# Query sketch of two batches through DRAM: one factor repeated by a read-back, the other on TensorE

## The chip, the core and the metric

The kernel runs on one core of a Trainium2 chip. A core has TensorE (PE in the profile; its weight loads are PEld), VectorE (DVE), ScalarE (ACT), GpSimd (POOL) and SyncE (SP), each with an instruction queue of its own that runs in order, and DMA queues that share 16 DMA engines. The metric is the time of one execution on the device in microseconds, as the median of several runs. Beside it stands one profiled execution with a trace of every instruction.

## The reference

```python
# q, k, v: (4 batches, 4 heads, 1088 tokens, 32), S1, S2: (8, 32)
def phi(x):                                # 32 numbers of a token become 64
    a = einsum('rd,bhsd->bhsr', S1, x)
    b = einsum('rd,bhsd->bhsr', S2, x)
    return einsum('bhsi,bhsj->bhsij', a, b).reshape(*x.shape[:-1], 64)
q_p, k_p = phi(q), phi(k)
kv = einsum('bhsf,bhsd->bhfd', k_p, v)
z = sum(k_p, axis=2)
num = einsum('bhsf,bhfd->bhsd', q_p, kv)
den = einsum('bhsf,bhf->bhs', q_p, z)[..., None] + 1e-6
x = (num / den).transpose(0, 2, 1, 3).reshape(4352, 128)
out = maximum(x @ w_in, 0)**2 @ w_out      # w_in 128x2048, w_out 2048x128
```

A linear attention with a sketch of degree two, and a feed-forward net (FFN) with the square of a ReLU on its result. All of it is one kernel.

## The kernel before

The four batches (b = 0 to 3 in the code, batches 1 to 4 in words) go one after the other through the attention, and the FFN works on tiles of 512 or 256 tokens as soon as these have passed it. Much of the attention of one batch therefore lies among FFN work of the batches ahead.

**Attention of a batch.** `kin`, `qin`, `vin` and `vtl` are loaded from DRAM. Those of batch 1 come in pieces on the queues of SP and ACT. All others, and the weights `w_in` and `w_out` in four pieces each, come through POOL (L360). DVE transposes `kin` to `kT` (L476) and `qin` to `qT` (L562). PE multiplies `kT` by `SK`, the sketch matrices (L496, a buffer `a` or `h`); ACT copies the first factor to `ka` (L509), and `kb` for POOL (L511); DVE or POOL forms all 64 products of a token, `kp` (L521). PE sums `kp` times `vp` over the tokens (L538). `vp` is `vin` with a column of ones, copied by ACT or POOL (L461, L464). Four copies put the sum into `kvz` (L553).

**The query side.** PE multiplies `qT` by `SR`, the sketch matrix with every row repeated eight times, once for each of the two factors (L583). Each factor thus arrives in PSUM already as 64 rows per head, one in the order 11112222 and one in the order 12341234. ACT copies the first factor to `A` (L598), since only one operand of the product is to come from PSUM, and DVE multiplies the other by it into `qp` (L609). PE forms `num`, with the sum for `den` in column 33 (L629). DVE adds eps (L647, L650), takes the reciprocal `rec` (L651) and multiplies it in, `xs` (L652, L656). PE transposes (L671), and DVE or ACT copies to `xT` (L677).

**FFN of a tile.** PE: `h` = `w_in` by `xT` (L698). ACT or DVE: `r` = relu(h) (L707, L709). DVE or ACT: `g` = r*r (L717, L715). PE: `o` sums `w_out` by `g` over all 2,048 inner rows (L724). DVE transposes to `osb` (L731), and SP stores (L741).

**Buffers.** PSUM holds three `h` of 1,024 columns, one `a` and one `o` of 512. SBUF holds four `r`, four `g`, three `osb`, three sets `den`/`rec`/`xs` and three `A`. Inputs of a batch have two sets, used in turn.

**Order.** The program is not written in order. Every piece is an operation with its engines, a duration that the author assumed, its inputs and its buffers. `Graph.run` plays these through once and emits the instructions in the order in which the operations start in that plan. Among operations that can start at about the same time a list `RANK` decides, and `SIDE` fixes the engine of those that could run on either. On the chip each engine then keeps that order and waits by semaphores.

**Loads.** A POOL load waits on a *gate*. The first (L346) is a one-column copy of the last piece of `vin` of batch 1. After that, the third load back must have landed: POOL copies one number of it to `gt` (L359). For batches 3 and 4 a further gate (L663) waits until the first `xs` of the batch ahead exists. 30 matmuls of zeros, `wz` (L325), fill PE before the data is there.

Of the kernel before, what the change touches and what calls it, by code (L numbers as in the profile page):

```python
# [9 lines left out]
F32 = mybir.dt.float32  # L10
# [9 lines left out]
DGE = 0.43  # L20


RANK = [
    165, 170, 191, 487, 140, 473, 83, 243, 387, 29, 569, 257, 275, 598, 621, 607, 623, 611, 618, 608, 596, 594,
    599, 602, 595, 610, 616, 617, 600, 605, 612, 614, 597, 609, 606, 603, 620, 619, 601, 613, 604, 622, 615,
    121, 85, 496, 286, 292, 31, 53, 582, 435, 476, 79, 120, 298, 526, 415, 475, 574, 355, 338, 160, 178, 10, 14,
    133, 365, 141, 57, 69, 104, 5, 2, 103, 126, 345, 26, 12, 306, 247, 314, 150, 9, 44, 152, 164, 71, 222, 4,
    74, 3, 55, 6, 100, 7, 93, 403, 182, 173, 507, 114, 539, 293, 76, 261, 80, 447, 384, 111, 215, 225, 366, 221,
    276, 299, 394, 17, 78, 92, 39, 145, 1, 135, 203, 193, 15, 98, 64, 52, 313, 382, 389, 357, 130, 369, 401,
    466, 212, 144, 579, 391, 370, 552, 456, 244, 518, 572, 327, 283, 498, 495, 530, 516, 262, 418, 591, 352,  # L30
    368, 564, 543, 485, 348, 477, 575, 316, 465, 302, 437, 542, 310, 188, 479, 201, 440, 49, 263, 147, 129, 199,
    67, 143, 11, 360, 367, 587, 511, 430, 450, 205, 541, 115, 59, 245, 464, 241, 482, 36, 171, 207, 444, 340,
    279, 537, 555, 218, 336, 86, 557, 109, 51, 554, 571, 66, 346, 406, 463, 264, 38, 489, 424, 124, 236, 25,
    250, 439, 371, 46, 350, 200, 392, 514, 154, 118, 8, 198, 18, 297, 206, 290, 524, 474, 462, 565, 592, 404,
    488, 139, 153, 142, 122, 374, 256, 134, 284, 27, 533, 81, 491, 535, 87, 556, 334, 443, 405, 106, 269, 326,
    268, 235, 540, 523, 503, 472, 460, 159, 578, 454, 397, 508, 558, 228, 41, 445, 509, 347, 23, 343, 300, 586,
    224, 291, 469, 471, 213, 28, 285, 20, 88, 50, 589, 77, 242, 33, 240, 132, 68, 398, 237, 204, 500, 90, 321,
    116, 515, 195, 289, 548, 303, 180, 184, 425, 412, 251, 234, 520, 429, 416, 156, 547, 329, 341, 317, 576,
    566, 560, 455, 502, 220, 380, 528, 480, 223, 181, 30, 32, 43, 75, 65, 166, 232, 22, 190, 499, 315, 97, 70,
    501, 72, 434, 127, 570, 417, 119, 158, 174, 373, 157, 253, 332, 484, 230, 214, 101, 532, 301, 238, 162, 216,  # L40
    231, 24, 378, 312, 172, 113, 358, 421, 82, 13, 359, 478, 529, 402, 255, 123, 442, 274, 61, 419, 559, 258,
    361, 45, 567, 536, 265, 525, 550, 545, 308, 395, 505, 583, 531, 325, 385, 590, 427, 335, 457, 110, 295, 519,
    561, 323, 544, 35, 73, 330, 62, 60, 233, 137, 91, 148, 63, 337, 48, 208, 95, 185, 146, 42, 458, 187, 112,
    167, 107, 163, 420, 58, 196, 287, 108, 149, 89, 362, 99, 331, 461, 383, 219, 410, 339, 483, 381, 273, 272,
    517, 259, 254, 436, 451, 534, 551, 319, 549, 584, 270, 356, 21, 453, 280, 490, 414, 553, 376, 521, 294, 396,
    581, 510, 513, 512, 282, 296, 426, 568, 131, 364, 438, 375, 94, 342, 136, 16, 278, 19, 209, 309, 486, 176,
    84, 56, 408, 177, 179, 493, 239, 105, 151, 311, 573, 40, 372, 432, 400, 47, 227, 192, 267, 102, 379, 328,
    585, 407, 377, 304, 506, 422, 563, 271, 189, 305, 527, 96, 428, 459, 186, 117, 217, 522, 37, 54, 388, 288,
    333, 210, 468, 399, 494, 229, 318, 183, 175, 249, 349, 413, 393, 277, 128, 562, 169, 252, 260, 497, 441,
    449, 588, 577, 593, 324, 246, 467, 452, 281, 322, 34, 492, 226, 307, 344, 125, 138, 353, 248, 538, 446, 433,  # L50
    155, 0, 431, 211, 390, 202, 351, 363, 386, 580, 546, 470, 409, 354, 481, 197, 423, 320, 411, 448, 266, 168,
    194, 504, 161,
# [3 lines left out]
    10: 1, 72: 1, 73: 0, 74: 1, 88: 1, 93: 1, 94: 0, 95: 1, 121: 1, 130: 0, 132: 0, 151: 0, 152: 1, 153: 0,  # L56
    174: 1, 178: 0, 187: 1, 188: 1, 202: 1, 207: 0, 208: 0, 209: 1, 210: 1, 234: 0, 242: 1, 244: 0, 258: 1,
    263: 1, 264: 1, 266: 0, 285: 0, 289: 1, 292: 1, 295: 0, 299: 1, 300: 1, 303: 0, 304: 0, 312: 1, 313: 0,
    316: 0, 317: 0, 320: 1, 324: 0, 328: 0, 329: 0, 332: 0, 333: 0, 336: 0, 337: 1, 341: 1, 349: 0, 350: 0,
    353: 0, 357: 0, 358: 0, 361: 0, 362: 1, 365: 0, 369: 0, 370: 0, 373: 1, 374: 0, 378: 1, 390: 0, 391: 1,  # L60
    395: 1, 398: 1, 399: 0, 403: 1, 406: 0, 407: 1, 410: 1, 411: 1, 414: 0, 415: 0, 418: 1, 419: 0, 427: 0,
    436: 1, 439: 0, 440: 0, 443: 0, 444: 0, 447: 0, 448: 0, 452: 0, 456: 1, 468: 0, 469: 0, 473: 1, 476: 0,
    480: 0, 481: 0, 484: 1, 485: 0, 488: 1, 492: 0, 496: 0, 505: 0, 506: 0, 509: 0, 510: 0, 513: 0, 518: 1,
    522: 1, 525: 0, 529: 0, 530: 0, 533: 1, 534: 0, 555: 1, 558: 0, 559: 0, 562: 0, 563: 0, 566: 0, 567: 1,
    571: 0, 574: 1, 584: 0, 587: 0, 592: 0, 595: 1, 604: 0, 608: 0, 609: 0, 613: 0, 616: 0, 617: 1,
# [10 lines left out]
class Op:  # L76
    def __init__(self, name, alts, fn, deps, pri, alloc, uses, port, dma, after, extra):
        self.extra = extra
        self.name, self.alts, self.fn, self.pri = name, alts, fn, pri
        self.deps = [d for d in deps if d is not None]  # L80
        self.alloc, self.uses, self.port, self.dma = alloc, uses, port, dma
        self.after = [d for d in after if d is not None]
        self.look = LOOK
        self.start = self.end = self.eng = None


class Graph:
# [22 lines left out]
    def run(self):  # L110
        eng_free, port_free, pipe, dge = {}, 0.0, 0.0, 0.0
        lanes = []
        todo = {id(o): len(o.deps) + len(o.after) for o in self.ops}
# [6 lines left out]
        while ready:  # L120
            cands = []
            for o in ready:
# [13 lines left out]
                for e, (busy, lat, *pen) in o.alts.items():  # L136
                    pen = pen[0] if pen else 0.0
                    t = max(eng_free.get(e, 0.0), t_slot)
# [30 lines left out]
            eng_free[e] = t + busy  # L169
            if e in o.port:  # L170
                port_free = t + busy
# [32 lines left out]
def kernel(  # L204
# [25 lines left out]

    def T(name, shape, dt=F32):
        return sb.tile(shape, dt, name=name, tag=name)
# [42 lines left out]
    kb = T("kb", [128, 2, H, R])  # L275
    kp = [T(f"kp{i}", [128, NJ, H, F]) for i in range(NB)]
    kvz = [[T(f"kvz{i}{x}", [128, 2, 2, D + 1]) for x in range(2)] for i in range(NB)]
    qp = [T(f"qp{i}", [128, 2, S]) for i in range(NB)]

# [39 lines left out]

    o_wz = add("wz", {"DVE": dve(256)}, lambda e: nc.vector.memset(wz, 0.0), pri=-150)  # L320
    wb = Buf("o")
    o_warm = o_wz
    for n in range(30):
        def f(e, n=n):
            nc.tensor.matmul(tiles["o"][0][:, 0:512], wz[:, 0:128], wz, start=True, stop=True)  # L325
        o_warm = add(f"warm{n}", {"PE": (0.4 if n < 6 else 0.215, 0.42 if n < 6 else 0.23)}, f, [o_warm], 1000,
                     alloc=[] if n else [wb], uses=[wb] if n else [])
    z_ops = []
# [15 lines left out]
    gateb = T("gateb", [128, 1], BF16)  # L344
    gt = T("gt", [1, 2])
    o_gate = add("gate", {"POOL": (0.1, 0.15)}, lambda e: nc.gpsimd.tensor_copy(gate[96:128], vin[0][96:128, H - 1, 7, D - 1 : D]), [z_ops[0]], -45)  # L346
    gated = [o_gate]
    chain = []

    def cload(name, dst, src, probe, pri, dma, deps=(), new=True):  # L350
# [6 lines left out]
        def f(e):  # L357
            if mark:
                nc.gpsimd.tensor_copy(gt[:, 0:1], mark[1])  # L359
            nc.gpsimd.dma_start(out=dst, in_=src)  # L360
        o = add(name, {"POOL": (0.85 if mark else 0.6, 3.0)}, f, gated + list(deps) + ([before[0]] if before else []), pri, dma=dma,
                after=[last[0]] if last else [])
# [49 lines left out]
    def attention(b, vt):  # L412
# [16 lines left out]
        if b == 0:  # L429
            o_kh = [[add(f"ldk{b}.{c0}", SPQ, ld(kin[i], k, c0, c1), (), -230 + c0 / 8, dma=1.85 * (c1 - c0) / 34)] for c0, c1 in ((0, 16), (16, 34))]  # L430
            o_k, o_k2 = o_kh[0][0], o_kh[1][0]
            o_q = [add(f"ldq{b}.{c0}", SPQ, ld(qin[i], q, c0, c1), (), -227 + 2 * c0, dma=2.0 * (c1 - c0) / 34) for c0, c1 in QS]
# [13 lines left out]
            o_gate.deps += o_v[1]  # L446
        else:
            if b > 1:
                load_k(b, vt(0) - 30, hist[(b, "gate")])
                load_v(b, vt(0) - 29)  # L450
                load_q(b, vt(0) - 28)
# [31 lines left out]
        JP = ((0, 2), (2, 4), (4, 7), (7, 9))  # L483
# [3 lines left out]
        for part, (j0, j1) in enumerate(JP):  # L487
# [10 lines left out]
            new = part in (0, 2)  # L498
# [5 lines left out]
        for part, (j0, j1) in enumerate(JP):  # L504
# [3 lines left out]
            def f_ka(e, j0=j0, j1=j1, n=n, q0=q0, qn=qn):  # L508
                nc.scalar.copy(ka[:, j0:j1].rearrange("p j h r -> p (j h r)"), at(kbuf[n])[:, 32 * (j0 - q0) : 32 * (j1 - q0)])  # L509
                if j1 == NJ:  # L510
                    nc.scalar.copy(kb.rearrange("p j h r -> p (j h r)"), at(kbuf[n])[:, qn + 32 * (j0 - q0) : qn + 32 * (j1 - q0)])  # L511
            o_ka = add(f"ka{b}.{part}", {"ACT": (0.22, 0.35) if j1 == NJ else act(32 * nj)}, f_ka, [ksks[part]] + hist.get((b - 1, "kprod"), []),
                       vt(3 + part) - kc, uses=[kbuf[n]])

            def f_kp(e, j0=j0, j1=j1, n=n, q0=q0, qn=qn):
                m = 4 * (j1 - j0)
                if e == "POOL":
                    bb = kb.rearrange("p j h r -> p (j h) r")
# [8 lines left out]
            o_kp = add(f"kp{b}.{part}", {"DVE": dve(256 * nj, fix=0.065)} | ({"POOL": (1.25, 1.35)} if j1 == NJ else {}), f_kp, [o_ka] + prev(b, "kv"),  # L527
                       vt(4 + part) - kc, uses=[kbuf[n]])
            mine("kprod", o_kp)
            prods.append(o_kp)  # L530
        kvb = Buf("a", "h")
# [35 lines left out]
        for u, (base, n, xs_) in enumerate(  # L567
                ((0, 256, (0, 1)), (512, 256, (0, 1)), (1024, 64, (0,))) if b else
                ((0, 128, (0, 1)), (256, 256, (0, 1)), (768, 128, (0, 1)), (1024, 64, (0,)))):
            hb = [Buf("h") for _ in xs_]  # L570

            def f_m(e, hb=hb, base=base, n=n, xs_=xs_):
                for ab in range(2):
# [237 lines left out]
```

## Time and profile before

| | |
|---|---|
| median of 13 runs | 120.58 us (119.98 to 121.9) |
| the profiled execution | 120.3 us, of which the span of the trace is 118.5 us |
| PE / PEld busy | 108.6 us (92%) / 67.0 us (57%) |
| DVE / ACT / POOL busy | 96.6 us (81%) / 92.0 us (78%) / 30.3 us (26%) |
| granted clock of TensorE | 0.999 |
| DMA | 10.19 MB, mean 86 GB/s |
| L583, query sketch on PE | 352 records |
| L598, copies to A on ACT | 22, 10.0 us |
| L609, products qp on DVE | 22, 11.9 us |
| L647 and L650, eps on DVE | 12, 2.0 us |

A float32 matmul leaves two records in the trace, so L583's 176 instructions show as 352. A busy PE is not PE at its peak, as matmuls are pipelined and overlap. Idle time of an engine counts only where the engine is what others wait for. The names on the left of an arrow are written, those on the right read.

### The profile page before, as it was taken

The numbers are of one execution on the slowest core, as the hardware profiler recorded it, in microseconds if no ns is written. First come the engines' busy times: TensorE is split into PE (matmuls) and PEld (weight loads), VectorE is DVE, ScalarE is ACT, GpSimd is POOL, SyncE is SP. The second block draws the span as 40 slices with busy tenths as digits, with TensorE's granted clock in tenths as the row PEclk, the third lists the DMA queues.
The fourth block names the chain that finished last, engine by engine and source line by source line (L and its number), as shares of the span: only waits on it lengthen the run. The fifth ranks groups of instructions, "written<-read, shape, count | busy, mean of one in ns | idle before, by whom it ended". The sixth has DMA issues, their size and how long they took to land.

```text
span 118.5 us, 3582 instructions
## 1 busy us (share of the span) xinstructions
PE 108.6 (92%) x1442; PEld 67.0 (57%) x1460; DVE 96.6 (81%) x179; ACT 92.0 (78%) x140; POOL 30.3 (26%) x73
## 2 busy tenths in 40 slices
PE   5999998999999998999999998999899999999850
PEld 2368566666756654554766545447656444567640
DVE  2569479989959699998559999999689989999920
ACT  0442367699986799999997999998639999999910
POOL 6129245576000665600005633300000000000000
PEclk9999999999999999999999999999999999999999
DMA  3970868775020099600311975102300050040522
GB/s 108 280 177 6 144 171 121 101 199 196 15 37 6 21 300 166 174 0 8 62 24 14 283 193 145 23 2 37 61 0 0 3 89 8 6 77 6 89 44 44
DMA packets 22272, 10.19 MB, mean 86 GB/s; under 512 B 19008, under 2 KB 20672, under 8 KB 22256
## 3 DMA queue, kind: packets, MB, share of 16 engines
q0 software_dynamic: 2688, 6.06, 20.8%
q1 hardware_dynamic: 18560, 3.54, 15.1%
q10 hardware_dynamic: 1008, 0.36, 1.4%
q8 instruction: 11, 0.18, 0.7%
q14 instruction: 5, 0.04, 0.1%
HBM read 8.78 MB, written 2.23 MB: 93 GB/s over the span
## 4 chain that ended last, share of the span: by engine, by line
PE 41%; ACT 18%; DMA 14%; DVE 12%; issue 9%; POOL 2%; DVEq 0%; ACTq 0%; POOLq 0%
PE o L724 15%; PE h L698 13%; ACT r L707 12%; DMA kin<-in_k_dram 7%; DVE g L717 6%; PE h L629 6%; DMA vin<-in_v_dram 4%; DMA w_in<-in_moe_w_in_dram 3%; ACT g L715 3%; PE h L583 2%; DVE qp L609 2%; ACT A L598 1%; PE a L496 1%; PE a L538 1%; DVE r L709 1%
## 5 line engine op out<-in xcount | busy, mean ns | idle before, releaser
L707 ACT ACTIVATE r<-h 128x1024 bf16<-128x1024 f32 x53 | 52.0, 1045 | 4.0 <-PE h L698 3.3
L698 PE MATMUL h<-xT,w_in 128*128 128x512 bf16 (+1 forms) x152 | 36.2, 348 | 1.1 <-ACT r L707 0.7
L724 PE MATMUL o<-g,w_out 128*128 128x512 bf16 (+1 forms) x154 | 33.7, 346 | 1.5 <-DVE osb L731 0.5
L717 DVE TENSOR_TENSOR g<-r 128x1024 bf16<-128x1024 bf16 x46 | 30.6, 696 | 1.0 <-ACT r L707 0.6
L715 ACT ACTIVATE g<-r 128x1024 bf16<-128x1024 bf16 x22 | 23.7, 1088 | 0.2
L698 PEld LDWEIGHTS <-w_in 128*128 128x128 bf16 x160 | 16.6, 115 | 12.7 <-issue 3.1
L724 PEld LDWEIGHTS <-w_out 128*128 128x128 bf16 x160 | 15.1, 98 | 13.4 <-issue 1.6
L709 DVE TENSOR_SCALAR r<-h 128x1024 bf16<-128x1024 f32 x15 | 18.0, 1210 | 1.2 <-PE h L698 1.2
L609 DVE TENSOR_TENSOR qp<-h,A 128x512 f32<-128x512 f32 (+2 forms) x22 | 11.9, 562 | 2.9 <-ACT A L598 2.8
L598 ACT COPY A<-h 128x512 f32<-128x512 f32 (+2 forms) x22 | 10.0, 504 | 4.8 <-PE h L583 4.6
L629 PEld LDWEIGHTS h<-kvz,qp 128*64 128x64 f32 x288 | 9.2, 137 | 3.6 <-DVE qp L609 2.0
L583 PE MATMUL h<-qT,SR 32*64 32x256 f32 (+2 forms) x352 | 10.9, 338 | 0.3 <-ACT r L707 0.3
L629 PE MATMUL h<-kvz,qp 128*64 128x66 f32 x288 | 10.4, 225 | 0.4 <-DVE kvz L553 0.2
L325 PE MATMUL o<-wz 128*128 128x512 bf16 x26 | 9.0, 468 | 1.5 <-DVE mk L288 1.2
L538 PEld LDWEIGHTS a<-vp,kp 128*64 128x64 f32 x216 | 6.9, 138 | 2.7 <-issue 2.2
L583 PEld LDWEIGHTS h<-qT,SR 32*64 32x64 f32 x352 | 6.4, 131 | 3.1 <-issue 0.5
L538 PE MATMUL a<-vp,kp 128*64 128x33 f32 x216 | 7.6, 224 | 0.1
L731 DVE STREAM_TRANSPOSE osb<-o 128x512 f32<-128x512 f32 (+1 forms) x10 | 6.3, 630 | 1.4 <-PE o L724 1.4
L663 POOL COPY gateb<-xs 128x1 bf16<-128x1 bf16 x3 | 0.6, 189 | 25.0 <-DVE xs L652 25.0
L360 POOL DMA_DIRECT2D vin<-in_v_dram x12 | 6.6, 561 | 0.4 <-issue 0.4
L476 DVE STREAM_TRANSPOSE kT<-kin 128x512 f32<-128x512 f32 x8 | 5.3, 682 | 1.4 <-DMA kin<-in_k_dram 1.4
L652 DVE TENSOR_TENSOR xs<-h,rec 128x512 bf16<-128x512 f32 (+2 forms) x9 | 5.8, 647 | 0.5
(65 smaller groups left out, 88.9 us busy)
## 6 DMA issues: line engine op xcount, KB each, us to landing
kin<-in_k_dram POOLq DMA_DIRECT2D x3, 544.0 KB, 4.3
qin<-in_q_dram POOLq DMA_DIRECT2D x3, 544.0 KB, 3.7
vin<-in_v_dram POOLq DMA_DIRECT2D x12, 128.0 KB, 4.2
out_dram<-osb SPq DMA_DIRECT2D x16, 64.0 KB, 1.9
w_in<-in_moe_w_in_dram POOLq DMA_DIRECT2D x4, 128.0 KB, 3.9
w_out<-in_moe_w_out_dram POOLq DMA_DIRECT2D x4, 128.0 KB, 3.9
qin<-in_q_dram SPq DMA_DIRECT2D x1, 416.0 KB
out_dram<-osb SPq DMA_DIRECT2D x10, 32.0 KB, 1.7
```

What stands on the lines that cost most here:

```text
L325: nc.tensor.matmul(tiles["o"][0][:, 0:512], wz[:, 0:128], wz, start=True, stop=True)
L538: nc.tensor.matmul(t[64 * (h % 2) : 64 * (h % 2) + 64, 33 * (h // 2) : 33 * (h // 2) + 33], kp[i][:, j, h, :], vp[i][:, h, j, :], start=(j ...
L583: nc.tensor.matmul(at(hb[x])[64 * y : 64 * y + 64, c0 : c0 + n], SR[32 * h : 32 * h + 32, ab].rearrange("p x y -> p (x y)"), rhs, start=Tr ...
L598: nc.scalar.copy(at(sA)[:, 0 : 2 * n].rearrange("p (r s) -> p r s", s=n), src(ab=0))
L609: nc.vector.tensor_tensor(out=o, in0=i0, in1=i1, op=ALU.mult)
L629: nc.tensor.matmul(at(nb)[64 * hf : 64 * hf + 64, col(x, pr)], qp[i][:, pr, n0 : n0 + 64], kvz[i][xx % 2][:, pr].rearrange("p y d -> p (y ...
L698: nc.tensor.matmul(at(hb)[:, step * w : step * w + N], w_in[:, 512 * (ct // E) : 512 * (ct // E) + 512].rearrange("p (c e) -> p e c", e=E) ...
L707: nc.scalar.activation(o, view(at(hb)), ACTF.Relu)
L709: nc.vector.tensor_scalar_max(o, view(at(hb)), 0.0)
L715: nc.scalar.activation(at(gb)[:, 0 : W * N], r, ACTF.Square)
L717: nc.vector.tensor_tensor(out=at(gb)[:, 0 : W * N], in0=r, in1=r, op=ALU.mult)
L724: nc.tensor.matmul(at(ob)[:, 0:N], w_out[:, ct, :], at(gb)[:, N * w : N * w + N], start=(ct == 0), stop=(ct == CT - 1))
```

## The change

The query side of batches 3 and 4 (b > 1) is computed in another way:

- The **first factor** is multiplied out without repeats, by a small matrix `SKD` built from `SK` (three POOL copies), into 128 rows of 272 numbers; ACT or DVE copies it to `As`; SP writes it to a DRAM tile `Aw`, and SP reads it back in two DMAs to `Ar`, each row eight times. No copies to `A` are made for these batches.
- The **second factor** is still multiplied out with repeats, by `SR`, in instructions of 512 columns, and DVE multiplies it by `Ar` into `qp`, 1,024 columns at a time.
- **Loads of batch 4** wait for both `Ar` of batch 3 (two copies to `gt`). The gates on `xs` are gone, batch 3 has none, and a batch's order is q, k, v instead of k, v, q. The first gate reads the first piece of `qin` in place of `vin`.
- **eps** is added by ACT (an Identity activation with a bias), between `num` and the reciprocal. `kp` comes in three products in place of four in batches 2 to 4, and the POOL one covers three blocks of tokens.
- **The plan**: a cost for PE's change between kinds of matmul (`SWITCH`), other durations of loads, and new `RANK` and `SIDE`. So all engines' orders differ from before.

```diff
+    As = [T(f"As{i}", [128, 272]) for i in range(NB)]
+    Ar = [T(f"Ar{i}", [128, 2, S]) for i in range(NB)]
+    Aw = [dr.tile([2, 2, R, S], F32, name=f"Aw{i}", tag=f"Aw{i}") for i in range(NB)]
+    SKD = T("SKD", [128, 2, 2, 2, R])
...
+    def f_SKD(e):
+        t = SK[:, 0].rearrange("p (r y) c -> p r y c", y=2)
+        nc.gpsimd.tensor_copy(SKD[:, 0], t)
+        for y in range(2):
+            nc.gpsimd.tensor_copy(SKD[:, 1, :, y], t[:, :, 1 - y])
...
-    o_gate = add("gate", {"POOL": (0.1, 0.15)}, lambda e: nc.gpsimd.tensor_copy(gate[96:128], vin[0][96:128, H - 1, 7, D - 1 : D]), [z_ops[0]], -45)
+    o_gate = add("gate", {"POOL": (0.1, 0.15)}, lambda e: nc.gpsimd.tensor_copy(gate[96:128], qin[0][96:128, 0:1]), pri=-45)
...
-                load_k(b, vt(0) - 30, hist[(b, "gate")])
-                load_v(b, vt(0) - 29)
-                load_q(b, vt(0) - 28)
+                wait = []
+                if b == 3:
+                    def f_gt(e):
+                        for pr in range(2):
+                            nc.gpsimd.tensor_copy(gt[:, 1:2], Ar[0][0:1, pr, 0:1])
+                    wait = [add(f"gate{b}", {"POOL": (0.3, 0.4)}, f_gt, hist[(2, "ar")], vt(0) - 31)]
+                load_q(b, vt(0) - 30, wait)
+                load_k(b, vt(0) - 29, wait)
+                load_v(b, vt(0) - 28, wait)
...
-        JP = ((0, 2), (2, 4), (4, 7), (7, 9))
+        JP = ((0, 4), (4, 6), (6, 9)) if b else ((0, 2), (2, 4), (4, 7), (7, 9))
...
+        if b > 1:
+            ab_ = Buf("a", "h")
+            def f_A(e):
+                w = lambda x: SKD[:, x].rearrange("p r y c -> p (r y c)")
+                for g in range(4):
+                    nc.tensor.matmul(at(ab_)[32 * g : 32 * g + 32, 0:256], w(g // 2), qT[i][:, 256 * g : 256 * g + 256], start=True, stop=True)
+                for g in range(4):
+                    nc.tensor.matmul(at(ab_)[32 * g : 32 * g + 32, 256:272], w(0), qT[i][:, 1024 + 16 * g : 1040 + 16 * g], start=True, stop=True)
...
+            o_As = add(f"As{b}", {"ACT": act(272), "DVE": dve(272)}, lambda e: (nc.scalar.copy if e == "ACT" else nc.vector.tensor_copy)(
+                As[i], at(ab_)[:, 0:272]), [o_A] + prev(b, "aw"), vt(5), uses=[ab_])
+            o_aw = add(f"aw{b}", {"SP": (0.6, 3.0)}, lambda e: nc.sync.dma_start(
+                out=Aw[i].rearrange("r y j (g s) -> g (r y j) s", g=4), in_=As[i]), [o_As] + prev(b, "ar"), vt(5.5), dma=0.4, extra=2.8)
...
+            for pr in range(2):
+                def f_ar(e, pr=pr):
+                    nc.sync.dma_start(out=Ar[i][:, pr, :], in_=Aw[i][pr].rearrange("y j s -> (y j) s")[:, None, :].to_broadcast([16, R, S]))
+                o_ar.append(add(f"ar{b}.{pr}", {"SP": (0.5, 3.0)}, f_ar, [o_aw] + prev(b, "qp"), vt(6), dma=3.0, extra=1.5))
...
+            def f_m(e):
+                for x in range(2):
+                    for h in range(H):
+                        pr, y = h // 2, (h + x) % 2
+                        nc.tensor.matmul(
+                            at(hb[x])[64 * y : 64 * y + 64, 512 * pr : 512 * pr + 512],
+                            SR[32 * h : 32 * h + 32, 1].rearrange("p x y -> p (x y)"), qT[i][32 * h : 32 * h + 32, 512 * x : 512 * x + 512],
+                            start=True, stop=True)
...
+            for x in range(2):
+                def f_qp(e, x=x):
+                    nc.vector.tensor_tensor(
+                        out=qp[i][:, :, 512 * x : 512 * x + 512].rearrange("p r (g s) -> p r g s", g=2),
+                        in0=at(hb[x]).rearrange("p (r g s) -> p r g s", r=2, g=2), in1=Av[:, :, 2 * x : 2 * x + 2, 0:256], op=ALU.mult)
...
+        else:
+            parts = ((0, 128, (0, 1)), (256, 256, (0, 1)), (768, 128, (0, 1)), (1024, 64, (0,)))
+            if b:
+                parts = ((0, 256, (0, 1)), (512, 256, (0, 1)), (1024, 64, (0,)))
...
-                nc.vector.tensor_scalar_add(dn_, v4[:, :, :, D], eps)
...
-                    nc.vector.tensor_scalar_add(den[:, 16:20], v5[:, :, D], eps)
+                if e == "ACT":
+                    nc.scalar.activation(dn_, v4[:, :, :, D], ACTF.Identity, bias=epsT[:, 0:1])
+                    if nx == 5:
+                        nc.scalar.activation(den[:, 16:20], v5[:, :, D], ACTF.Identity, bias=epsT[:, 0:1])
+                    return
```

## The prediction

> **What bounds the kernel now.** I read the page's busy shares first, then the table of ten-microsecond stretches, then the engines in order of time for the first 25 us, then the groups by form and the longest waits.
>
> ```profile
> PE 108.6 (92%) x1442; PEld 67.0 (57%) x1460; DVE 96.6 (81%) x179; ACT 92.0 (78%) x140; POOL 30.3 (26%) x73
> ```
>
> ```profile
> 10.00:20.00 10.00, 9.20 (x207) 6.52 (x207) 7.32 (x21) 4.60 (x11) 5.21 (x13) 1.00 0.63 119
> ...
> 60.00:70.00 10.00, 9.95 (x113) 5.95 (x112) 8.77 (x17) 8.93 (x12) 4.44 (x11) 1.00 0.49 123
> ...
> 80.00:90.00 10.00, 9.68 (x210) 6.88 (x212) 8.37 (x17) 6.71 (x11) 0.00 (x0) 1.00 0.17 29
> 90.00:100.00 10.00, 9.95 (x49) 4.88 (x50) 9.53 (x17) 9.86 (x11) 0.00 (x0) 1.00 0.16 30
> ```
>
> After the two times the columns are PE, PEld, DVE, ACT, POOL, granted clock, DMA share, GB/s. From 20 us on three engines are nearly full together, so no single one can be relieved with profit; between 80 and 90 us ACT has 3.3 us free while PE works through attention. Only before 20 us are ACT and DVE slack, and there the transfers set the pace:
>
> ```profile
> 9.42 1.06 POOL L521 TENSOR_TENSOR kp<-kb,ka 128x512 f32<-128x512 f32 x1
> 10.55 0.19 POOL L346 COPY gate<-vin 32x1 f32<-32x1 f32 x1
> 10.68 0.77 POOL L360 DMA_DIRECT2D w_in<-in_moe_w_in_dram  x1
> 11.44 0.55 POOL L360 DMA_DIRECT2D w_out<-in_moe_w_out_dram  x1
> 11.97 0.55 POOL L360 DMA_DIRECT2D kin<-in_k_dram  x1
> ```
>
> ```profile
> 17.12 0.71 DVE L476 STREAM_TRANSPOSE kT<-kin 128x512 f32<-128x512 f32 x1 [0.82 <-DMA kin<-in_k_dram]
> ```
>
> The first weight load is issued at 10.68, behind a copy of vin and a product on POOL; the keys of the second batch leave at 11.97 and DVE can transpose them at 17.12.
>
> **What the Trainium skill says.** (1) "Trainium Kernel Development and Optimization", section Performance Expectations: matmul busy time is a poor measure, since matmuls overlap. The trace agrees: a 512-column record has a mean of 382 ns at L698, yet the chain lists pairs at 0.43 us, 0.215 each. So the 92% is not 92% of the array. (2) "DMA: Bandwidth & Descriptors", Anatomy of one DMA: about 2 us of a transfer are fixed. The trace agrees roughly: 64 KB stores land 1.9 us after issue. (3) The same page, Bandwidth: 1 MB took 6.15 us of engine time on the GpSimd queue; no transfer of that size is in this trace, and the new one is on SP's queue. (4) "TensorEngine Tiling (Array Packing)", Key Properties: a change of tiling mode drains TensorE. No view of before isolates that.
>
> **The change, part by part.** Counts are instructions in the two programs, durations are means of the profile of before.
>
> PE. For batches 3 and 4 the old sketch L583 is two sets of 16 instructions of 256 columns and 8 of 64. The chain gives 1.14 us for one set (32 records) and 0.39 for the small set: 2.6 us per batch with 1.1 per set. The new one has 8 of 512 columns (the columns of one set: 1.1) and 4 of 64 (0.2), plus 8 with SKD: four of 256 columns, four of 16. That form is not in the trace. Its 1,024 columns cost 0.28 at the old set's rate (4,096 in 1.1); as four column groups can run together where the old form had eight places, I double that and add a little for the small ones: 0.6, with 0.3 and 1.1 as bounds. Saving 0.7 per batch, bounds 0.2 and 1.0: **1.4 us in all**. The rest of PE's instructions are the same in number.
>
> ACT. Copies to A: 8 of 607 ns and 2 of 265 go, -5.4. One As copy comes, +0.4 (the 256-wide copy is 382 ns). Twelve additions of eps come from DVE; the nearest ACT instructions of that size, SR and kvz, take 0.21, so +2.4. The planner's sides change: r 53 to 51, -2.1; g 22 to 26, +4.35. Smaller copies (ka, kb, vp tail, xT, SR, kvz) together -1.8. **Sum -2.2 us.**
>
> DVE. den -2.0 (L647 1.5, L650 0.5). g 46 to 42, -2.8; r 15 to 17, +2.4. qp: eight of 685 ns become four of twice the width, 1.22 each by the slope of the 128-, 256- and 512-wide rows, -0.6. kp: 9.2 becomes 9.6, +0.4, because POOL's four products of 512 become two of 768 (1.6 each by the row of 1,066 ns). As, SR, one more xT, one kvz less: +0.9. **Sum -1.7 us.**
>
> Start. The gate no longer reads vin but the first piece of q, which DVE transposes at 6.36 without a wait. The POOL order is now SKD (three copies of about 0.2 after SK, 6.4), gate, w_in, w_out, one vp copy, kin. So w_in goes out near 7.2 instead of 10.68 and kin near 9.3 instead of 11.97: 2.7 us earlier. Every following load hangs on probes of these, so they shift too. What is it worth? From 9.14 to 22.44 DVE idles only 0.32 + 0.55 + 0.56 + 0.61 + 0.82 = 2.9 us, and the last kp product of batch 1 now lies on DVE ahead of the second transposition of q (+0.65), SR ahead of SK (+0.2). The first den steps leave DVE (-0.5). I take **1.0 us gained**, bounds 0 and 2.7.
>
> The round trip. A3 on PE, As, Aw (139 KB to DRAM, about 2 us), then two reads of 557 KB each in which every row is read eight times: 1.11 MB. Estimate from the DMA page 6.8 + 2 us; from the 194 GB/s that the stretch 40 to 50 reaches, 5.7 + 2. With the write and the hand-overs 10 to 11 us. In DVE's new order between the As copy of batch 3 and the first qp that reads Ar stand 8 g, 3 r, 2 qp, 2 kp, 2 output transposes and 8 smaller ones, by the rows some 16 us. In batch 4 ACT has 13 r and 7 g, about 20 us, between As and the next den. I cost the trip at nothing: that work hides it. If the cover goes, each microsecond past 16 stops DVE at qp and all g and r behind it, to which PE and ACT answer at once. On SP the six DMAs stand between stores of outputs; a store may land some 10 us later, and three osb buffers cover that. In traffic 2.5 MB are added to 10.2, in a stage with DMA shares of 0.1 to 0.8: nothing, up to 1 us if loads of k and v collide.
>
> The new gate. Batch 4's loads wait for both Ar reads, and in POOL's queue they stand behind the kp product of batch 3, which waits for kb on ACT. I put that near 49 us (DVE's As at about 35, 12 to 14 us of listed work). In the old trace these loads left at 63.75, so they are still earlier: nothing, with about 3 us of cover before DVE wants qT of batch 4.
>
> The sum. In the full stretch 20 to 112 us the three busy engines lose 1.4, 2.2 and 1.7; what all can give is the least, 1.4. With 1.0 at the start: -2.4 on the profiled execution's 120.3 (span 118.5, 1.8 outside it), that is 117.9. The median of the thirteen runs is 0.28 above that execution: **118.2 us**. The tail is unchanged: last 16 matmuls 1.91, a transpose of 0.45, stores.
>
> **The rivals.** *Slower: the new hop.* num on PE now goes to ACT for eps and only then to DVE for the reciprocal, nine times, and ACT is a queue of instructions of 1.05 to 1.09 us. A hop costs half of such an instruction, 0.2 for the addition and about 0.1 to be told, less DVE's old 0.16: 0.6 us, 5.6 in all. Fully exposed that gives 120.6 - 2.4 + 5.6 = 123.8, half exposed 121.0. It decides from 0.27 us per group. For it: DVE already waits for num (L647, 2.4 us in three waits). Against it: FFN work of earlier tiles stands between, and only a group whose xT is needed at once shows it. A late Ar at qp is the second form of a stall on DVE; it needs a trip over 16 us, which I hold unlikely. *No change:* the end is set by where PE waits, not by its work, and the start is eaten by DVE: 120.0 to 121.2. For it, three engines stay full to the tenth. *Much faster:* the start gives its whole 2.7 and the stage 80 to 90 closes: 120.6 - 2.7 - 2.0 = 115.9. *It doesn't do what it says:* if the planner sent qp or den elsewhere, counts would differ; the program shows that they moved as told.
>
> **Numbers.** Forecast 117 to 119.5: 0.56. Much faster, 115.5 to 117: 0.17. No change: 0.10. Slower: 0.17. A run of this kernel can tell 0.5%, 0.6 us, from nothing. Faster by more than that 0.73, within it 0.09, slower 0.18. The range 115.9 to 121.2 takes in the forecast, most of the faster case and the mild half of the hop; the faster cases alone would give 115.9 to 119.5.
>
> **What would show it.** Right: w_in issued near 7 us, kT of batch 2 before 15; Ar landed before qp (no DVE wait on Ar above 0.3 us), sums of PE, DVE and ACT down by the amounts above, eight wide copies fewer at L598, and xs waiting little for ACT. Wrong: DVE waits named rec<-ACT den over 0.3 us a group, qp<-DMA Ar, or a PE stretch below 9 of 10 between 30 and 110 us.

## The result and the profile after

The changed kernel's median is 118.69 us (117.93 to 119.45, 11 runs), beside 120.62 us for the kernel before on the same chips. The ratio is 0.985, with a 95% interval of 0.9825 to 0.9875: **1.8 us faster** (1.5 to 2.1). The profiled execution took 117.96 us with a span of 116.2, so its sum stands 0.7 below the median, and differences of profiles below about 1 us are not read as differences of the kernels: from the first transposition of q to the first FFN matmul, nine programs with the same instructions up to there took 10.8 to 11.8 us in their profiles. Ratios leave out executions in a slower state, more than 1.5% above the fastest of the same kernel: none of the changed kernel, but 11 of 22 with the late gate, 4 of 10 with the doubled read-back and 4 of 6 with the old sketch, so that these three differences are rather too small.

The page's busy line of the kernel after:

```profile
PE 106.6 (92%) x1363; PEld 65.4 (56%) x1380; DVE 95.1 (82%) x162; ACT 91.2 (78%) x139; POOL 30.2 (26%) x76
```

PE lost 2.0 us, DVE 1.5, ACT only 0.8. The span lost 2.3. PE's idle time is nearly what it was, 9.6 us for 9.9. PE's total is rough: this trace has 1,363 of 1,380 records, and in traces that have all 1,380 of the same PE program, such as those with more for ACT or DVE below, PE is busy for 108.8 to 109.5 us. The ten-microsecond stretches that were shown of the kernel before (columns: PE, PEld, DVE, ACT, POOL, clock, DMA share, GB/s):

```profile
10.00:20.00 10.00, 9.38 (x245) 7.18 (x248) 6.86 (x16) 5.32 (x14) 3.82 (x10) 1.00 0.79 139
...
60.00:70.00 10.00, 9.57 (x145) 5.79 (x145) 7.48 (x14) 9.31 (x18) 2.76 (x7) 1.00 0.50 130
...
80.00:90.00 10.00, 9.54 (x125) 5.29 (x125) 9.06 (x16) 7.98 (x11) 0.00 (x0) 1.00 0.16 28
90.00:100.00 10.00, 9.89 (x47) 4.67 (x47) 9.23 (x12) 9.88 (x12) 0.00 (x0) 1.00 0.16 28
```

Between 80 and 90 us ACT does 1.3 us more than before and PE has 125 records in place of 210: less attention, more FFN. POOL's order of time at the start, and DVE's a little later:

```profile
6.47 0.18 POOL L368 COPY gate<-qin 32x1 f32<-32x1 f32 x1
6.88 0.77 POOL L384 DMA_DIRECT2D w_in<-in_moe_w_in_dram  x1 [0.23 <-issue]
7.65 0.57 POOL L384 DMA_DIRECT2D w_out<-in_moe_w_out_dram  x1
8.26 0.61 POOL L491 COPY vp<-vin 128x512 f32<-128x512 f32 x1
8.82 0.53 POOL L384 DMA_DIRECT2D kin<-in_k_dram  x1
```

```profile
14.65 0.20 DVE L751 RECIPROCAL rec<-den 128x8 f32<-128x8 f32 x1 [1.37 <-ACT den L747]
14.96 0.42 DVE L752 TENSOR_TENSOR xs<-a,rec 128x256 bf16<-128x256 f32 x1
15.30 0.70 DVE L506 STREAM_TRANSPOSE kT<-kin 128x512 f32<-128x512 f32 x1
...
19.07 0.25 DVE L751 RECIPROCAL rec<-den 128x16 f32<-128x16 f32 x1 [0.83 <-ACT den L747]
```

The loads leave as forecast, w_in at 6.88 and kin at 8.82. The keys of batch 2 are transposed at 15.30 (before 17.12) with no wait for a DMA. In front of that DVE waits 1.37 us for ACT's addition of eps, the new hop; how much of that wait is the hop's own is asked below. The first FFN matmul is later than before (17.03 to 15.77 us), the first transposition to osb earlier (29.10 to 30.74).

The largest shift between the two programs lies between 70 and 90 us. Groups of PE in that stretch, first of the kernel before, then after (busy us and mean ns after the bar):

```profile
L698 PE MATMUL h<-xT,w_in 128*128 128x512 bf16 x21 | 6.3, 385 | 0.4 <-ACT r L707 0.3
L724 PE MATMUL o<-g,w_out 128*128 128x512 bf16 x22 | 5.7, 380 | 0.3 <-issue 0.2
L583 PE MATMUL h<-qT,SR 32*64 32x256 f32 (+1 forms) x80 | 2.7, 355 | 0.0
...
L496 PE MATMUL a<-SK,kT 128*64 128x64 f32 x16 | 0.9, 234 | 0.0
L496 PE MATMUL h<-SK,kT 128*64 128x64 f32 x20 | 0.8, 222 | 0.0
```

```profile
L794 PE MATMUL h<-xT,w_in 128*128 128x512 bf16 x31 | 8.7, 381 | 0.1
L820 PE MATMUL o<-g,w_out 128*128 128x512 bf16 x29 | 7.6, 379 | 0.1
...
L629 PE MATMUL h<-qT,SR 32*64 32x512 f32 x16 | 1.1, 613 | 0.3 <-ACT r L803 0.3
...
L648 PE MATMUL h<-qT,SR 32*64 32x64 f32 x8 | 0.3, 241 | 0.1
```

FFN work in these 20 us is 16.3 us instead of 12.0. The query sketch is 1.4 us here instead of 2.7, and the key sketch of batch 4 (1.7) is gone from here: its loads leave POOL at 53.5 to 58.3 us, where they left at 63.75 and later, so it is done before 70.

### The profile page after: what moved, and what is told of

Same layout as the page of the kernel before. It is cut to its first block, busy times and chain, and to the rows that moved or that the text cites. A ratio compares the mean times of both kernels' runs of the same rounds, so it can differ in the third digit from the quotient of the medians.

```text
span 116.2 us, 3420 instructions
## 1 busy us (share of the span) xinstructions
PE 106.6 (92%) x1363; PEld 65.4 (56%) x1380; DVE 95.1 (82%) x162; ACT 91.2 (78%) x139; POOL 30.2 (26%) x76
## 4 chain that ended last, share of the span: by engine, by line
PE 66%; ACT 13%; DVE 9%; issue 4%; DMA 2%; another core or an unknown queue 1%; ACTq 0%; DVEq 0%
PE h L794 20%; PE o L820 19%; PE h L726 7%; ACT r L803 6%; ACT g L811 4%; PE a L571 4%; PE h L680 4%; DVE kp L551 3%; DMA S_sb<-in_S_dram 2%; DVE r L805 2%; PE h L629 2%; PE h L571 2%; PE o L346 2%; PE a L526 2%; DVE xs L752 1%
## 5 line engine op out<-in xcount | busy, mean ns | idle before, releaser
L803 ACT ACTIVATE r<-h 128x1024 bf16<-128x1024 f32 x51 | 49.8, 1033 | 3.9 <-PE h L794 3.2
L813 DVE TENSOR_TENSOR g<-r 128x1024 bf16<-128x1024 bf16 x42 | 27.8, 679 | 3.7 <-ACT r L803 2.0
L811 ACT ACTIVATE g<-r 128x1024 bf16<-128x1024 bf16 x26 | 27.3, 1071 | 0.6 <-PE o L820 0.3
L805 DVE TENSOR_SCALAR r<-h 128x1024 bf16<-128x1024 f32 x17 | 20.5, 1215 | 0.2
L695 ACT COPY A<-h 128x512 f32<-128x512 f32 (+2 forms) x12 | 5.0, 468 | 3.6 <-PE h L680 3.6
L706 DVE TENSOR_TENSOR qp<-h,A 128x512 f32<-128x512 f32 (+2 forms) x12 | 6.0, 528 | 1.5 <-ACT A L695 1.3
L551 POOL TENSOR_TENSOR kp<-kb,ka 128x768 f32<-128x768 f32 x2 | 3.2, 1592 | 14.4 <-ACT ka L539 13.2
L752 DVE TENSOR_TENSOR xs<-h,rec 128x512 bf16<-128x512 f32 (+1 forms) x8 | 5.4, 675 | 0.6
L751 DVE RECIPROCAL rec<-den 128x16 f32<-128x16 f32 (+3 forms) x9 | 2.2, 249 | 4.4 <-ACT den L747 4.0
L595 DVE STREAM_TRANSPOSE qT<-qin 128x512 f32<-128x512 f32 (+3 forms) x8 | 5.5, 718 | 0.4 <-DMA qin<-in_q_dram 0.4
```

The lines of the kernel that those rows point to most:

```text
L551: (nc.gpsimd if e == "POOL" else nc.vector).tensor_tensor(out=kp[i][:, j0:j1].rearrange("p j h (x y) -> p (j h) x y", y=R), in0=bb[:, :, N ...
L752: nc.vector.tensor_tensor(out=xs[:, 0 : min(nx, 4)].rearrange("p (y x) (h d) -> p y (x h) d", y=y, d=D), in0=v4[:, :, :, 0:D], in1=rc_[:, ...
L803: nc.scalar.activation(o, view(at(hb)), ACTF.Relu)
L805: nc.vector.tensor_scalar_max(o, view(at(hb)), 0.0)
L811: nc.scalar.activation(at(gb)[:, 0 : W * N], r, ACTF.Square)
L813: nc.vector.tensor_tensor(out=at(gb)[:, 0 : W * N], in0=r, in1=r, op=ALU.mult)
```

## The experiments

All ratios are against runs of the kernel before on the same chip. Where two ratios are subtracted, the interval is the root of the sum of the two squared half-widths, and 1% is 1.2 us.

**The start alone, and its absence.** The first kernel is the one before with the early gate and nothing else:

```diff
-    ... nc.gpsimd.tensor_copy(gate[96:128], vin[0][96:128, H - 1, 7, D - 1 : D]) ...
+    ... nc.gpsimd.tensor_copy(gate[96:128], qin[0][96:128, 0:1]) ...
+    move(["gate", "w_in0", "w_out0"], "ident"); move(["ldk1"], "vp0.0"); move(["gate1"], "ldq1")
```

> The kernel before with the start of the changed one alone: the first gate reads the first piece of q, gate and first weights stand ahead of the POOL copies of vin, the keys of batch 2 after the first copy; the unused gate of batch 2 moves behind its loads. All else is as before. If the start is worth what I summed, 1.0 us: 119.6. If it is eaten by DVE: 120.4 to 120.8. If the shift of the loads counts whole: 118.5 or less.

Measured: 0.9973 (0.995 to 0.9996), 0.3 us faster (0.05 to 0.6). The second is the changed kernel with the gate made late:

```diff
-    ... nc.gpsimd.tensor_copy(gate[96:128], qin[0][96:128, 0:1]) ...
+    ... nc.gpsimd.tensor_copy(gate[96:128], kp[0][96:128, 8, 3, 63:64]) ...
+    move([gate and the loads that stood before the last kp of batch 1], last_kp)
```

> The changed kernel with the first gate put back to its old time: it reads the last product kp of batch 1 (ready near 10.6 us) in place of the first piece of q, and the POOL copy of vin stays ahead of it, so the weights and the keys of batch 2 leave about 3.5 to 4 us later, near their old times. All else, the order of every other engine too, is as in the changed kernel. If the start gave what I summed (1.0 us), this is 119.7. If the start is eaten by DVE (rival: no change from it), it stays at 118.7. If the loads' shift counts whole (rival: much faster start), it is 121 or more.

Measured: 1.0052 (1.0019 to 1.0084), which is 2.4 us (1.9 to 2.9) slower than the changed kernel, slower even than the one before. DVE and PE of this kernel in order of time, and a stretch just after:

```profile
15.57 0.20 DVE L751 RECIPROCAL rec<-den 128x8 f32<-128x8 f32 x1 [1.37 <-ACT den L747]
15.88 0.42 DVE L752 TENSOR_TENSOR xs<-a,rec 128x256 bf16<-128x256 f32 x1
18.53 0.71 DVE L506 STREAM_TRANSPOSE kT<-kin 128x512 f32<-128x512 f32 x1 [2.22 <-DMA kin<-in_k_dram]
```

```profile
20.09 0.95 PE L794 MATMUL h<-xT,w_in 128*128 128x256 bf16 x4 [2.31 <-DVE qp L706]
```

```profile
20.20:23.60 3.40, 3.40 (x52) 2.93 (x51) 1.40 (x4) 1.57 (x3) 1.24 (x3) 0.50 0.75 102
```

So loads that leave earlier are worth 0.3 us in one order, and loads that leave later cost 2.4 in the other. The two edits are not of one size. On the old order w_in left 3.9 us earlier (6.75 instead of 10.68). In the second kernel it left 5.3 us later than in the changed one (12.22 instead of 6.88), and so 1.5 later than in the kernel before; what a gate at just the old time would cost was not run.

Why the first number is small is not shown. In that kernel the first FFN matmul comes at 16.29 instead of 15.77, but DVE is already 0.6 later at its first kp product (8.16 instead of 7.53, where it waits for ACT's ka), so this may be the scatter of the profiles. The second number has a chain in its trace. In the changed order kT stands in front of three qp products, so a late kin stops these too, and PE waits 2.31 us for qp before its first FFN matmul. The execution traced took 122.46 us, and behind PE's pause its granted clock was 0.50 for 3.4 us, so a part of the loss may be the clock's.

**The hop num, ACT, DVE.** eps goes back to DVE, in all nine groups, or in the first alone together with the first copy to xT:

```diff
+    EPS_DVE = {all nine (b, x0)}          # second kernel: {(0, 0)}
...
-                if e == "ACT":
+                if e == "ACT" and (b, x0) not in EPS_DVE:
...
+                if (b, x0) in EPS_DVE:
+                    nc.vector.tensor_scalar_add(dn_, v4[:, :, :, D], eps)
```

> The changed kernel with eps added by DVE again, directly ahead of the reciprocal, in all nine groups; ACT adds none. ACT loses 3.2 us of instructions, DVE gains 2.0. If the new hop costs nothing (my sum), DVE's 2.0 us more make it slower: 119.5 to 120.5. If the hop costs (the rival on the slower side, DVE waits of 4.0 us for den in the trace), it is faster: 117 to 118. About equal, 118.4 to 119, if both cancel.

> The changed kernel with two steps of the first group alone back on DVE: eps of batch 1's first group, and its copy to xT, both on ACT behind three copies to A in the trace (DVE waits 1.4 us for den, the first FFN matmul starts at 17.0 against 15.8 before). If the first group's chain sets the start, the first FFN matmul comes near 16 us and the time falls by 0.5 to 1: 117.7 to 118.2. If the start is set by loads or by the sum of work, the first matmul comes earlier and the time stays at 118.5 to 118.9.

Measured: 0.9847 (0.98 to 0.9893) and 0.9829 (0.9786 to 0.9872), beside 0.985. Neither differs from the changed kernel (0.0 and -0.3 us, each within 0.6). In the first, ACT has 1.8 us less and DVE 1.8 us more to do. That a gain and a loss cancel here is unlikely, as 2.0 us more of DVE's squares cost 0.1 below, but no run excludes it. DVE's waits in the changed kernel, then in the first of these two:

```profile
DVE rec L751 <- ACT den L747: 4.0, 3, 1.8
```

```profile
DVE den L755 <- PE h L727: 1.8, 2, 1.3
DVE den L755 <- PE a L727: 1.1, 1, 1.1
```

After each name stand the total in us, the number of waits and the longest. Without the hop DVE still waits 2.9 us in three waits, now for PE's num. Most of the 4.0 us is thus a wait for num that bears ACT's name, and the hop's own share is small. In the second kernel the first FFN matmul did not come earlier, as was hoped: it stands 12.0 us behind the first transposition of q, where it is 10.8 to 11.8 in the changed kernel and the programs that start like it. That run therefore says nothing about what an earlier first group would be worth.

**The round trip made longer.** Each read-back is issued twice, then three times, into the same tile:

```diff
+                    for _ in range(2):    # 3 in the second kernel
                         nc.sync.dma_start(out=Ar[i][:, pr, :], in_=Aw[i][pr]...to_broadcast([16, R, S]))
```

> The changed kernel with each read of Ar issued twice: 2.2 MB more traffic in all, and Ar lands some 5 to 6 us later (near 52 and 79 us where DVE wants it at 54.8 and 81.9). My step (the trip costs nothing under a cover of 16 us) expects no change, 118.4 to 119.0. If traffic that collides with the loads costs, or stores behind it on SP: 119.3 or more.

> The changed kernel with each read of Ar issued three times: Ar would land some 11 us later, near 58 and 84 us, past the places where DVE wants it. The cover is then gone in batch 3 by about 3 us and in batch 4 by about 2, and batch 4's loads leave about 5 us later. If each microsecond past the cover stops the others, +3 to +6: 122 to 125. If the queues behind have slack of their own: under +1.5.

Measured: 1.0102 (1.0054 to 1.0149) and 1.1867 (1.1816 to 1.1919), that is 3.0 us (2.4 to 3.7) and 24.3 us (23.6 to 25.0) over the changed kernel. The first was expected to cost nothing and the second 3 to 6. A second read of a tile waits on SP until the first has landed, so the reads don't overlap: SP waits 19.3 us for them in four waits. DVE in the kernel with two, and then with three reads:

```profile
57.37 1.23 DVE L638 TENSOR_TENSOR qp<-h,Ar 128x1024 f32<-128x1024 f32 x1 [1.53 <-DMA Ar<-Aw]
...
87.51 1.22 DVE L638 TENSOR_TENSOR qp<-h,Ar 128x1024 f32<-128x1024 f32 x1 [1.66 <-DMA Ar<-Aw]
```

```profile
66.75 1.23 DVE L638 TENSOR_TENSOR qp<-h,Ar 128x1024 f32<-128x1024 f32 x1 [11.51 <-DMA Ar<-Aw]
...
105.25 1.23 DVE L638 TENSOR_TENSOR qp<-h,Ar 128x1024 f32<-128x1024 f32 x1 [10.29 <-issue]
```

The profile names no releaser for the last of these waits; the last read of Ar, issued at 100.47, landed at 105.17. With three reads, 21.8 us of wait stand beside 24.3 us lost, about one for one. With two reads no such price can be read: the 3.2 us of wait come from an execution of 124.05 us, 6.1 over the profiled one of the changed kernel, while the ratio gives 3.0. The gate on Ar opens later too (POOL waits 3.2 us for it in the kernel with two reads, 13.1 with three), and these runs don't part it from DVE's wait. The clock may have a part in what goes beyond the wait. In the stretch 60 to 70 us of the kernel with three reads PE stands still and its clock is halved, and in that with two it was 0.50 from 61.3 to 64.7:

```profile
60.00:70.00 10.00, 1.64 (x3) 0.41 (x3) 2.77 (x4) 0.40 (x3) 1.56 (x5) 0.50 0.66 133
```

**Doses.** If the three engines pace the kernel together, an added microsecond should show on each. Some PE products, some ACT relus (384 of 1,024 columns) and some DVE squares of the middle tiles are done twice. Each addition stands directly in front of the operation that it repeats, so the doses of the three engines stand at different places:

```diff
         for o in order:
+            if o.name in {"m1.2.2", "m1.3.3", "m1.4.2", "m1.5.1", "m1.6.1"}: o.fn(o.eng)    # PE
+            if o.name in {"r.2.2", "r.3.3", "r.4.2", "r.5.1"}: o.fn("ACT+")                 # ACT
+            if o.name in {"g.2.4", "g.4.4", "g.6.3"}: o.fn(o.eng)                           # DVE
             o.fn(o.eng)
```

> The changed kernel with 2.15 us of PE work added: five pairs of FFN matmuls (512 columns, in tiles 3 to 7, between 40 and 100 us) are done twice into the same buffer, 0.43 us each. It asks what a microsecond of PE is worth in the full stretch. My step (what all can give is PE's saving) expects +1.8 to +2.2. If the three engines share the bound: +0.7 to +1.5. If PE waits for others most of the time: under +0.5.

> The changed kernel with 2.0 us of ACT work added: in four places in the same tiles, ACT does 384 columns of a relu once more, 0.5 us each. My step expects that ACT is not the bound there: under +0.7. If the three engines share the bound: +0.7 to +1.5. If ACT is the bound: +1.8 to +2.2.

> The changed kernel with 2.0 us of DVE work added: three squares g of 1,024 columns in tiles 3, 5 and 7 done twice, 0.68 us each. My step expects under +0.7; a shared bound +0.7 to +1.5; DVE as the bound +1.8 to +2.2.

> The changed kernel with all three additions at once: 2.15 us on PE, 2.0 on ACT, 2.0 on DVE. If the busiest engine sets the time (my step), the additions lie beside one another: +2.0 to +2.4. If each engine's work is paid for in its own place along one chain (rival: the chain adds up), the sum of the three single results, which would be more than +2.5.

| dose | ratio (95%) | against the changed kernel |
|---|---|---|
| PE, 2.15 us | 0.9891 (0.9856 to 0.9926) | +0.5 us, within 0.5 |
| ACT, 2.0 us | 0.9985 (0.9961 to 1.0008) | +1.6 us, within 0.4 |
| DVE, 2.0 us | 0.9856 (0.982 to 0.9893) | +0.1 us, within 0.5 |
| all three | 1.0083 (1.0053 to 1.0113) | +2.8 us, within 0.5 |

The three are not equal: at these places ACT's dose is paid at 0.8 us per us, PE's at 0.2 (just at the edge of the noise), and DVE's at nothing that shows. All three together cost 2.8 us and the single ones 2.2 in sum, within 0.9; whether they add up or go beyond the sum is not decided.

**Less for ACT.** If it is the amount of ACT's work that is priced, taking some away should gain. Four squares go from ACT to DVE:

```diff
         for o in order:
-            o.fn(o.eng)
+            o.fn("DVE" if o.name in ("g.2.3", "g.3.5", "g.4.3", "g.5.0") else o.eng)
```

> The changed kernel, with four squares g of 1,024 columns (one each in the third to sixth FFN tiles, near where the dose for ACT stood) done by DVE in place of ACT. By the trace of the changed kernel an ACT square takes 1.06 us and a DVE one 0.66, so ACT loses 4.2 us and DVE gains 2.6. Theory A, the amount of ACT's work sets the pace (2.0 us more of it cost 1.6): 4.2 less bring 2 to 3.3 us, a ratio of 0.957 to 0.968 against the kernel before. Theory B, a dose on ACT costs because of the place it stood in, and taking work away elsewhere only lets the next engine set the pace: up to 0.5 us, 0.980 to 0.986. Theory C, DVE is the late one at these squares, since its queue gets each of them late: slower than the changed kernel by 0.5 to 2 us, 0.989 to 1.002.

Measured: 1.0059 (1.0035 to 1.0083), 2.5 us (2.1 to 2.9) slower than the changed kernel: the number of theory C, somewhat beyond its range. The largest single loss is in DVE's and POOL's order of time at 50 us:

```profile
50.27 3.29 DVE L813 TENSOR_TENSOR g<-r 128x1024 bf16<-128x1024 bf16 x3
53.48 0.68 DVE L551 TENSOR_TENSOR kp<-a,ka 128x512 f32<-128x512 f32 x1
```

```profile
51.51 1.50 POOL L551 TENSOR_TENSOR kp<-kb,ka 128x768 f32<-128x768 f32 x1 [13.09 <-ACT ka L539]
```

```profile
L813 DVE TENSOR_TENSOR g<-r x3: 682/684/1868, 50.3 to 51.7; 128x1024 bf16<-128x1024 bf16 x3
```

The last view gives the shortest, median and longest duration in ns. The third square, started at 51.7 beside POOL's product, took 1.87 us instead of 0.68. The osb transposition that follows is 1.6 us later, counted from the first FFN matmul, and the following tile loses another 0.6. So 1.2 us of the loss at this place is one square that ran longer beside POOL, which no theory had. The run rules out theory A, that the amount of ACT's work by itself sets the pace. It does not show what less work for ACT alone is worth, since DVE got that work; a kernel in which ACT's work goes away altogether was not run. That the price of ACT's dose belongs to the places where it stood is therefore likely but not shown.

**The old sketch at the new places.** In the changed kernel, batches 3 and 4 form both factors by SR with copies to A, in the emission order of the new ones, without the round trip. The second half of its products comes when one of its buffers has been given to another operation, so part of the computation is overwritten and PE waits for it.

```diff
-            f_A, As, Aw, Ar of batches 3 and 4
+            for ab in range(2): for x in range(2): for h in range(H):     # columns 0 to 511, then 512 to 1023
+                nc.tensor.matmul(at(hb[x])[...], SR[32 * h : 32 * h + 32, ab]..., rhs, start=True, stop=True)
+            nc.scalar.copy(A, ...) ; nc.vector.tensor_tensor(out=qp, in0=..., in1=A, op=ALU.mult)
```

> The changed kernel with the old query sketch of batches 3 and 4 at the new places: both factors repeated on PE, ACT copies to A, products of 512 columns; no As, Aw, Ar, no gate on Ar. All other orders as in the changed kernel. It adds 0.6 us of PE and about 2.3 us of ACT per batch, DVE about the same, and takes 2.5 MB of traffic away. By my step (the busiest engine's saving counts: PE) it is 1.2 to 1.5 slower than the changed kernel: 119.9 to 120.2. If ACT is what counts there: 121 to 123, and part of that is the new place of the copies, which no plan has arranged. If the sketch gave nothing: 118.4 to 119.

Measured: 1.0279 (1.0206 to 1.0352), 5.2 us (4.2 to 6.1) over the changed kernel, more than either theory gave. Its ratio rests on two executions. PE in order of time shows why the run does not price the sketch:

```profile
59.55 1.87 PE L799 MATMUL h<-xT,w_in 128*128 128x512 bf16 x4 [2.10 <-DVE qp L643]
61.35 1.87 PE L731 MATMUL h<-kvz,qp 128*64 128x66 f32 x40
```

PE waits 2.1 us for qp, and the instructions behind it take 1.87 us where they took 1.05 and 1.39; the granted clock was 0.50 from 59.0 to 62.4. The loss mixes a badly placed wait with a slower clock, and what the sketch is worth by itself stays open.

## Why the prediction was right, and where it was not

**The total** of 118.2 us against 118.69 is right, as are the start times of the loads and the round trip being hidden. It is right in part by luck: the rule that turned the three engines' savings into 1.4 us failed, and the 1.0 us of the start is not a gain of its own. Of the signs that it named, kT of batch 2 came at 15.30 and not before 15, and xs did wait for ACT.

**PE, -1.4.** The query sketch of batches 3 and 4 went from 5.2 us busy (2.5 and 2.7, L583) to 4.0: L629 and L648 2.7, L606 and L608 0.7 a batch (the estimate was 0.6). That is 1.1, so the term was a little too large. The form with SKD took 0.64 us for its eight records of 256 columns.

**ACT, -2.2.** The forecast counts instructions times their mean duration. Counted so it came to -2.4 (104.6 to 102.2 us), and the term holds. Busy time, which counts overlap once, fell by 0.8 only, as the instructions overlapped less than before. Within the sum the copies to A came as forecast (-5.5). Mis-sized were the additions of eps (255 to 275 ns each, not 0.21: +3.2 instead of +2.4) and, the other way, the squares (+3.9 instead of +4.35) and the relus (-2.7 instead of -2.1). For eps the nearest row was too short by a quarter.

**DVE, -1.7.** Counted so it was -2.4, in busy time -1.5. The 0.7 more lies in the squares (-3.5, not -2.8): the one square of 1.44 us in the trace before makes that difference.

**"What all can give is the least, 1.4."** This is the step that failed as a rule, though its number was near. By it, as the expectations of the doses say, a microsecond more on PE is paid in full and one on ACT or DVE hardly. The doses show it otherwise: ACT's extra work was paid at 0.8, PE's at 0.2, DVE's at nothing. With the 0.8 of ACT's busy time as the least, the rule would even give 118.8, closer than the forecast; that is a coincidence and no support. What holds in its place is narrower: equal doses on three nearly full engines cost 0.5, 1.6 and 0.1 us, and neither the busiest engine nor the sum of ACT's work says which. Whether the place in the order decides is not shown. The skill's warning that the prediction used ("Trainium Kernel Development and Optimization", Performance Expectations, on matmul busy time) is in keeping with this: 2.15 us more of PE's records cost about 0.5 us here, though the run does not show why.

**The start, -1.0, bounds 0 and 2.7.** The sum took it as a gain of its own. On the old order it is 0.3 us, although w_in left 3.9 us earlier there; so the reading that before 20 us the transfers set the pace does not hold for the kernel before. In the new order, with loads 5.3 us later than in the changed kernel, going without costs 2.4. The gain depends on the order around it, POOL's and DVE's, and cannot be added as one term.

**The round trip, nothing.** Right as it stands, and its cover was a little understated. In the trace after, DVE makes As of batch 3 at 36.23; the reads are issued from 40.31, and the one whose landing is on record lands 4.9 us later; qp begins at 54.76 without a wait for Ar. In batch 4 As begins at 62.23 and a read lands at 73.3. The trip is 9 to 11 us (10 to 11 forecast) and the cover 18.5 us (16 forecast); batch 4 has 19.6 us of cover from 62.23 to 81.87. That each microsecond past the cover is paid about one for one agrees with the kernel with three reads, in which the gate on Ar was late as well.

**The new gate, near 49 us.** The copies from Ar came at 53.0, but not for Ar: POOL stood at kp until 51.38, waiting 13.2 us for ACT's ka. The queries of batch 4 left at 53.48 and were transposed at 58.77 without a wait. Nothing was lost, and the sketch of batch 4's keys moved out of the stage 70 to 90.

**The rivals.** *The new hop* falls: the waits exist (1.37 us at the first group, above the 0.3 that the prediction named as a sign against it), yet with eps back on DVE the time is the same within 0.6 us. That sign was badly chosen: a wait named for ACT is for the most part PE's num, which DVE waits for without the hop as well (2.9 us; 2.4 in the kernel before). *No change* falls with the ratio. In *Much faster* the stage 80 to 90 was to close; ACT's 3.3 us free there became 2.0.

**Open.** How the 1.8 us divide between the smaller sketch, the earlier batch 4 and the order written for them is not shown. The one kernel meant to separate the sketch didn't, no kernel with less work for ACT alone was run, and no kernel with a newly planned order was tried.

## What to carry to other kernels

In a kernel with three nearly full engines, neither the busiest nor the least relieved could be shown to set the price of a microsecond; a small dose at the place in question measures it there and need not hold elsewhere. Moving work from one engine to another is not the opposite of a dose, since the second engine pays for it. A wait in the trace bears the name of the last link alone: take that link away and see which wait takes its place before calling it a cost. A transfer that is hidden should be judged by the distance between landing and use; where that was exceeded by far, the loss was about one for one. A part of a change can be nearly worthless by itself and worth more beside the rest, so test it in both directions, with edits of the same size: alone on the old kernel, and missing from the new.

## What was not expected of the hardware

- **DVE squares beside POOL.** Two bf16 squares of 1,024 columns (0.68 us) that started while a product of POOL was under way ended about 0.55 us after POOL was done: 1.87 us in the kernel with four squares moved (51.69, POOL's product ended at 53.01), 1.44 in the kernel before at 27.84 (POOL's product and the copy behind it ended at 28.73). It went the other way too: POOL's product of 128x768 took 1.67 us in the changed kernel, where at 51.38 it began 0.3 us before a square's end, but 1.51 at 25.21 and 1.50 in the kernel with four squares moved. DVE's r at 25.41 of the changed kernel, which reads PSUM, kept its 1.21 us beside POOL's product of 25.21. Issues of DMAs by POOL did not have this effect: the square at 53.52, beside the issue of 53.48, took 0.69. A square of 0.94 in the kernel with eps on DVE, at 27.96, stays unexplained. "VectorE: DVE Perf Modes", Two Vector instructions with no wait between them, says that the second SBUF read interface of DVE is shared with GpSimd; a square has two inputs in SBUF, and the two cases agree with it, though no run tested it alone.
- **Rows read eight times.** Of the four 544 KB read-backs, each row of DRAM read eight times on SP's queue, two have a landing on record, after 4.9 and 6.5 us; in the kernel with three reads ten of twelve landed in 4.4 to 6.8. Beside that stand medians of 4.9 for the loads of k and 3.8 for those of q, which have the same size. The write of 136 KB ahead of them took longer than forecast: SP issued it at 36.65 and the reads that wait for it at 40.31.
- **The clock after a pause of PE.** With the late gate PE stood still for 2.3 us from 17.78, and the granted clock was 0.50 from 20.2 to 23.6. With the old sketch it stood for 2.1 us from 57.45, and the clock was 0.50 from 59.0 to 62.4. With two reads it stood for 0.9 and 1.3 us within 3.2 us, and the clock was 0.50 from 61.3 to 64.7. With three reads the pauses were 10.9 and 9.7 us, and the clock was 0.50 for 13.7 and 10.2 us. Single pauses of 1.0 and 1.4 us were not followed by a drop, and the ten traces without a pause over 0.9 us show no drop before the last 2 us. What the slower clock added in these four kernels no run separates.
